# Early rows of a fourth expert, with weight loads and zero writes moved, in a fused attention and mixture-of-experts kernel

## The chip, the cores and the metric

One core of a Trainium2 chip runs the kernel. The metric is device time in microseconds (us): the median of the runs shown. Engines are called as the profile calls them: PE (matrix multiplication), DVE (vector), ACT (activations), POOL (GpSimd, which also issues the indirect transfers and those that change the data type) and SP (the sync engine, which issues plain transfers and nothing else here).

## What is computed

Linear attention over 8 batches of 576 tokens with 8 heads of 64, and on its output a layer of eight experts with noisy top-2 routing:

```python
phi = lambda x: np.where(x > 0, x, np.exp(x) - 1.0) + 1.0
q_p, k_p = phi(q), phi(k)
kv = np.einsum('bhsd,bhse->bhde', k_p, v);  z = np.sum(k_p, axis=2)
x = np.einsum('bhsd,bhde->bhse', q_p, kv) / (np.einsum('bhsd,bhd->bhs', q_p, z)[..., None] + 1e-06)
# x as 4608 tokens of 512
noisy = x @ w_gate + np.log1p(np.exp(x @ w_noise)) * noise     # 8 experts
top2, top2_w = two largest per token, softmax of the two
for e in range(8):                                             # w1[e] 512x1024, w2[e] 1024x512
    out[mask] += top2_w[mask] * (np.maximum(x[mask] @ w1[e], 0.0) @ w2[e])
```

## The kernel before

**Attention and routing.** Attention goes over four groups of two batches (g = 0 to 3). For each group the loads of q, k and v run on POOL's queue with a change to bf16 (`PhaseA.load`, L163); `exp` and `phi` make the features on ACT and DVE, `kv_mm` and `num` are the two products on PE. The tokens of a group are a routing unit; group 3 makes two, so there are five units (`UNITS`, L32). `rt_a`, `rt_b`, `rt_c` compute the two experts of every token, the weights and a row number, on DVE mostly.

**The lists.** Every expert has two lists of rows in a DRAM tensor, `x_sorted`: F, the tokens that visit it first (the lower of their two experts), and S, those that visit it second. `dispatch` (L391) writes the rows there: for each column of 128 tokens and each of the two experts one indirect transfer on POOL (L398), with a small memset behind it that keeps them apart (L389). That is 18 transfers for each of the units 0 to 2, 12 for unit 3 and 6 for unit 4. An F row's result goes to a tensor `part` (L661, on SP's queue); an S row's result is added to what `part` holds of the same token, gathered by POOL (L613, tile L), and scattered to the output (L667).

**Blocks.** The expert work is cut into tiles of 128 rows and blocks of one to four tiles. A block's rows are loaded on SP's queue (`xn_load`, L566, and a small `meta_load`, L449), transposed on PE (`xn_t`, L592) and copied by ACT (L596, L598); `mm1` (L630) makes the first product, in eight parts of 4 matmuls, ACT applies the relu (L632), and `mm2` (L645) the second, tile by tile; DVE scales the result (L649, L651). `interval` (L677) interleaves one block's first product with the second products of the block before and the transposes of the block after; behind it stand the gathers of L for the next block and, on POOL, the weight loads given to it (`w_load`, L442, one of the two matrices of an expert at a time). Each expert but the first and last also has 192 middle rows, at the border between its lists, whose place is known only at the end: `mid_gather` (L499) fetches them with two indirect transfers on POOL (L504, tile xm). M stands for these tiles in the plan.

**Early rows.** A list is complete only when unit 4 is dispatched. To have work for PE before, `ROUNDS` (L34) names, for three points (after units 0, 1 and 2), how many rows of the F lists of the first experts are full by then: at each point `rt_c` (L385) raises the row counters to these bounds, so that rows below them are never written later. Blocks below a bound are read as soon as the dispatches of that unit have landed: a load for round i takes the group number i (`early`, L550). Before the change the blocks are, in order, 0F0,2 in round 0; 0F2,2 and 1F0,3 in round 1; 0F4,2, 1F3,2 and 2F0,4 in round 2 (expert, list, first tile, number of tiles). Then comes c0, 0F6,4, the first block that needs the complete list, and the rest as in `PLAN` (L927).

**Orders.** The program is written out in the order in which every engine takes its instructions: `attention` (L758) has the groups and the first early blocks, `routing` (L883) the others, the kernel's main function (L939) the rest: at block i it prepares the expert of block i + 2 (`prepare`, L526: row data and the middle gather), loads rows two blocks ahead, and gives the weight loads of the table `todo` (L989) to the intervals. Weights lie in pools of two, three and one experts. Before the main loop nothing stands in PE's order but what these functions list.

**Zeros.** Some rows behind the lists are read without having been written; `attention` writes zeros there at its beginning, with seven transfers to `x_sorted` and two to `part` on SP's queue (L771 to L778).

Of the kernel before, what the change touches and what calls it, by code (L numbers as in the profile page):

```python
# [9 lines left out]
INT32 = mybir.dt.int32  # L10
# [23 lines left out]
ROUNDS = [(0, (256, 0, 0)), (1, (512, 384, 0)), (2, (768, 640, 512))]  # L34
EARLY = 3
# [14 lines left out]
def build_constants(tc, consts, w_gate, w_noise, noise):  # L50
# [23 lines left out]
    c["gap2"] = tile_("gap2", [P, 352])  # L74
# [337 lines left out]
class PhaseB:  # L412


    def __init__(self, ctx, tc, w1, w2, x_sorted, part, out):
# [11 lines left out]
        self.left, self.ready = [0] * 6 + [1] * 5 + [2] * 4, set()  # L427
# [16 lines left out]
    def meta_load(self, e, kind, i0, nt, group=None):  # L444

        m = self.mp.tile([P, nt, 4], INT32, name=f"meta{nt}{kind}")
# [310 lines left out]

def attention(pa, pb, c, x_sorted, zrow):  # L758
# [12 lines left out]
    nc.vector.memset(zrow[:], 0.0)  # L771

    for e, kind, i, n in ((0, "F", 8, 2 * P), (3, "F", 4, P), (4, "S", 4, P), (7, "S", 8, 2 * P), (E, "S", 0, 1)):
        row = pb.row(e, kind, i)
        for a in range(0, n, P):
            nc.sync.dma_start(out=x_sorted[row + a : row + min(n, a + P), :], in_=zrow[0 : min(P, n - a)])
    nc.sync.dma_start(out=pb.part[NO_P : NO_P + 1].bitcast(INT32)[:, 0 : ROW_W // 2], in_=zrow[0:1])
    nc.sync.dma_start(out=pb.part[NO_P : NO_P + 1].bitcast(INT32)[:, HD - ROW_W // 2 : HD], in_=zrow[0:1])  # L778
# [25 lines left out]
    for g in range(3):  # L804
# [4 lines left out]
        pa.phi(n, "k")  # L809
        if g < 2:  # L810
            pa.load(g + 2, "q")
# [42 lines left out]
        elif g == 1:  # L854
            for i in range(2):
                pa.dispatch(1, 3 * i, 3 * i + 3)
                pb.w_load(1, i)
            pa.dispatch(1, 6, 9)
            pb.xn_load(a1, 1)
            pb.meta_load(0, "F", 2, 2, 1)  # L860
            pb.meta_load(1, "F", 0, 3, 1)
        else:
            pa.dispatch(2)
# [19 lines left out]
def routing(pa, pb, c, first):  # L883
# [3 lines left out]
    a2, c0 = pb.block(2, ("F", 0, 4)), pb.block(0, ("F", 6, 4))  # L887
    pb.w_tiles(2, 1)
    pb.w_tiles(3, 1)
    pb.xn_load(a1, 1)  # L890
    pb.meta_load(0, "F", 4, 2, 2)
# [3 lines left out]
    pb.meta_load(2, "F", 0, 4, 2)  # L895
    pb.xn_load(a2, 2)
# [6 lines left out]
    pa.dispatch(3, 0, 3)  # L903
    pb.w_load(2, 0)
    pa.dispatch(3, 3, 6)
    pb.w_load(2, 1)
# [7 lines left out]
    pa.dispatch(4)  # L914
    pb.mids()
    pb.xn_t(b0, 0)
    pb.interval(b0, a1, (), b1)
    pb.prepare(0)
    pb.xn_load(c0)
    pb.interval(b1, b0, (), a2)  # L920
    pb.interval(a2, b1, (), c0)
    return a2, c0
# [123 lines left out]
```

## Time and profile before

| | |
|---|---|
| median of 9 runs | 448.85 us (442.62 to 453.0) |
| the profiled execution's own time | 447.72 us |
| its span, first to last instruction | 445.9 us |
| PE busy | 365.0 us, 82% of the span |
| POOL busy | 273.4 us, 61% |
| ACT, DVE busy | 194.1 us (44%), 183.6 us (41%) |
| mean granted clock of TensorE | 0.895 |
| first product, L630 | 832 matmuls, 150.0 us |
| second product, L645 | 640 matmuls, 147.4 us |
| dispatches, L398 | 72, 75.5 us of POOL |
| 16 weight loads, L442 | 1 MB each, 11.5 us from issue to landing (median) |

The profile is of one execution. Busy time is the time in which an engine works on an instruction; a time in the timelines counts from the first instruction. A line such as "b<-xt,w" names tiles by the program: the result is left of the arrow. The brackets behind an instruction of the timeline hold the idle time of its engine just before it and what ended it. A transfer has two times: the issue by its queue's engine, and the landing, when its semaphore tells that the data is there.

### The profile page before, as it was taken

How to read it: one execution, taken by the hardware profiler on the slowest of the kernel's cores; microseconds unless marked ns; L12 is line 12 of the kernel's file. 1: busy time of each engine (PE TensorE's matmuls, PEld its weight loads, DVE VectorE, ACT ScalarE, POOL GpSimd, SP SyncE). 2: the span in 40 equal slices, each digit the busy share in tenths (PEclk: the TensorE clock that was granted, in tenths of full speed). 3: DMA queues.
4: the chain of work that ended last, by engine and by line, in shares of the span. 5: the costliest groups of instructions: out<-in, count | busy, mean ns of one | idle time of the engine just before them, and what ended most of it. 6: DMA issues, size and time to landing. Idle time of an engine off the chain costs nothing.

```text
span 445.9 us, 7157 instructions
## 1 busy us (share of the span) xinstructions
PE 365.0 (82%) x2641; PEld 218.2 (49%) x2641; DVE 183.6 (41%) x471; ACT 194.1 (44%) x321; POOL 273.4 (61%) x408
## 2 busy tenths in 40 slices
PE   3593576474868779899999999799999899999990
PEld 1383465353645446445565445444645555554450
DVE  2746989998485722103423132312321141231230
ACT  1718654650624424353455534354444345445310
POOL 7120328988888887620084728268569846878781
PEclk9758856756788969999999999999999999999996
DMA  9999996599885399693387997977996996654440
GB/s 133 208 233 208 208 208 165 122 230 219 188 211 188 99 263 257 201 224 98 125 201 197 219 235 175 259 219 182 248 220 207 238 228 196 220 156 148 160 154 29
DMA packets 63010, 85.59 MB, mean 192 GB/s; under 512 B 15887, under 2 KB 45714, under 8 KB 62966
## 3 DMA queue, kind: packets, MB, share of 16 engines
q0 software_dynamic: 36160, 63.91, 64.6%
q1 hardware_dynamic: 25142, 20.96, 15.4%
q10 hardware_dynamic: 1664, 0.18, 0.5%
q8 instruction: 22, 0.36, 0.3%
q14 instruction: 22, 0.18, 0.1%
HBM read 83.88 MB, written 33.79 MB: 264 GB/s over the span
## 4 chain that ended last, share of the span: by engine, by line
PE 54%; DMA 21%; POOL 11%; DVE 6%; issue 4%; ACT 3%; POOLq 0%; SPq 0%; ACTq 0%; DVEq 0%
PE b L645 25%; PE b L630 24%; POOL x_sorted L398 7%; DMA kq<-in_q_dram 6%; DMA xm<-x_sorted,m_idx 5%; DMA xn<-x_sorted 4%; PE t L592 4%; DMA w<-in_moe_w_dram 3%; DMA kq<-in_k_dram 2%; POOL gap L389 2%; ACT e L178 1%; DMA x_sorted<-xr,posi 1%; ACT xt L596 1%; DVE e L190 1%; DVE xr L283 1%
## 5 line engine op out<-in xcount | busy, mean ns | idle before, releaser
L630 PE MATMUL b<-xt,w 128*128 128x256 bf16 (+5 forms) x832 | 150.0, 326 | 4.8 <-ACT xt L596 3.5
L645 PE MATMUL b<-w,hT 128*128 128x512 bf16 (+1 forms) x640 | 147.4, 386 | 0.0
L632 ACT ACTIVATE hT<-b 128x256 bf16<-128x256 f32 (+5 forms) x208 | 98.5, 484 | 101.4 <-PE b L630 99.1
L630 PEld LDWEIGHTS <-w 128*128 128x128 bf16 x832 | 79.8, 99 | 60.1 <-issue 9.2
L645 PEld LDWEIGHTS <-hT 128*128 128x128 bf16 (+1 forms) x640 | 59.7, 100 | 66.2 <-issue 5.7
L398 POOL DMA_INDIRECT x_sorted<-xr,posi x72 | 75.5, 1049 | 23.8 <-issue 11.9
L596 ACT COPY xt<-t 128x1024 bf16<-128x1024 bf16 x30 | 30.4, 1012 | 53.2 <-PE t L592 53.0
L613 POOL DMA_INDIRECT L<-part,mgi x12 | 12.0, 998 | 54.7 <-DMA xn<-x_sorted 30.9
L667 POOL DMA_INDIRECT out_dram<-y,si x34 | 33.7, 991 | 15.7 <-DVE y L649 11.5
L178 ACT ACTIVATE e<-kq 128x2304 bf16<-128x2304 bf16 x16 | 33.3, 2123 | 22.1 <-PE misc L209 9.3
L613 POOL DMA_INDIRECT L<-part,gi x34 | 34.7, 1020 | 6.9 <-issue 5.4
L209 PEld LDWEIGHTS <-e 64*128 64x128 bf16 x288 | 22.3, 128 | 17.3 <-DVE e L190 13.1
L209 PE MATMUL b<-v,e 64*128 64x192 bf16 x144 | 20.8, 323 | 8.9 <-DVE e L190 5.8
L592 PE MATMUL t<-ident,xn 128*128 128x128 bf16 (+1 forms) x256 | 21.0, 221 | 6.8 <-DMA xn<-x_sorted 5.7
L272 PE MATMUL num<-kvbd,pqt 128*64 128x162 bf16 x288 | 17.8, 294 | 10.4 <-DVE lwt L290 9.6
L209 PE MATMUL misc<-v,e 64*128 64x192 bf16 x144 | 20.7, 323 | 5.5 <-DMA v<-in_v_dram 5.5
L592 PEld LDWEIGHTS <-xn 128*128 128x128 bf16 (+1 forms) x256 | 17.2, 99 | 15.6 <-DMA xn<-x_sorted 7.0
L283 DVE TENSOR_TENSOR xr<-num,rden 128x768 bf16<-128x768 f32 x24 | 21.9, 952 | 2.2 <-DMA x_sorted<-xr,posi 1.5
L667 POOL DMA_INDIRECT out_dram<-y,msi x12 | 11.7, 976 | 16.3 <-DVE y L649 8.6
L190 DVE TENSOR_TENSOR e<-e,kq 128x2304 bf16<-128x2304 bf16 x16 | 21.5, 1357 | 0.3
L651 DVE TENSOR_SCALAR y<-b,meta2F 128x512 f32<-128x512 f32 x14 | 10.4, 749 | 27.0 <-PE b L645 26.9
L272 PEld LDWEIGHTS <-pqt 128*64 128x64 bf16 x288 | 14.9, 143 | 13.0 <-DVE lwt L290 7.6
(170 smaller groups left out, 358.8 us busy)
## 6 DMA issues: line engine op xcount, KB each, us to landing
w<-in_moe_w_dram POOLq DMA_DIRECT2D x16, 1024.0 KB, 11.5
part<-y SPq DMA_DIRECT2D x39, 256.0 KB, 3.6
kq<-in_k_dram POOLq DMA_DIRECT2D x8, 576.0 KB, 20.1
kq<-in_q_dram POOLq DMA_DIRECT2D x8, 576.0 KB, 13.1
v<-in_v_dram POOLq DMA_DIRECT2D x8, 576.0 KB, 23.0
xn<-x_sorted SPq DMA_DIRECT2D x11, 256.0 KB, 4.6
xn<-x_sorted SPq DMA_DIRECT2D x6, 384.0 KB, 4.6
xn<-x_sorted SPq DMA_DIRECT2D x4, 512.0 KB, 7.2
```

What stands on the lines that cost most here:

```text
L178: self.nc.scalar.activation(out=e, in_=x, func=ACT.Exp)
L209: nc.tensor.matmul(out=self.kvps[g, h, j][:, KVM * i : KVM * i + KVM], lhsT=e[half, hp, ci, :], rhs=v[half, hp::4, 64 * ci : 64 * ci + 64] ...
L272: nc.tensor.matmul(out=ps[half, hp, KVW * i : KVW * i + KVW], lhsT=self.pqt[g, 3 * t + i][:, hp, half], rhs=self.kvbd[g][:, j, hp, :], sta ...
L283: nc.vector.tensor_tensor(out=_ap(xr, [[64, 4], [ROW_W, 3], [1, 64]], off=3 * t * ROW_W + 256 * s), in0=_ap(ps, [[512, 4], [KVW, 3], [1, 6 ...
L398: r = self.nc.gpsimd.indirect_dma_start(out=self.x_sorted, out_offset=bass.IndirectOffsetOnAxis(ap=self.r["posi", u][:, ci - c0, sl : sl + ...
L592: nc.tensor.transpose(ps[:, i, dc, 0:m], self.xn(b, t, dc), self.c["ident"][0:m, 0:m])
L596: nc.scalar.copy(out=b["xt"][:, :, t * P : t * P + 2 * P].rearrange("p c (i r) -> p i c r", i=2), in_=ps)
L613: r = nc.gpsimd.indirect_dma_start(out=L[0:m].bitcast(INT32), out_offset=None, in_=self.part.bitcast(INT32), in_offset=bass.IndirectOffset ...
L630: nc.tensor.matmul(out=ps[:, 0:n], lhsT=w1[:, dc, fc * P : fc * P + P], rhs=b["xt"][:, dc, 0:n], start=(dc == 0), stop=(dc == 3))
L632: nc.scalar.activation(out=b["hT"][:, fc, 0:n], in_=ps[:, 0:n], func=ACT.Relu)
L645: nc.tensor.matmul(out=ps[i * m : i * m + m], lhsT=b["hT"][:, f, t * P : t * P + m], rhs=w2[:, f, :], start=(fc == 0), stop=(fc == 8 // n ...
L667: r = nc.gpsimd.indirect_dma_start(out=self.out, out_offset=bass.IndirectOffsetOnAxis(ap=self.m[e, kind, i]["si"][0:m], axis=0), in_=y[0:m ...
```

## The change

It does these things:

- Round bounds for a fourth expert: 256 rows of expert 2 in round 1 already, and 384 of expert 3 in round 2.
- The early blocks after 1F0,3 become 2F0,2 (round 1), 0F4,2, 1F3,2, 2F2,2 and 3F0,3 (round 2). The block 2F0,4 is split in two, and the first three tiles of expert 3 move from behind the blocks of expert 2 to a place ahead of c0. Expert 3's plan loses a 4-tile block and has 3F3,2, then M,S,M, then S1,2.
- The loads of rows for 2F0,2 and 0F4,2, 1F3,2 are issued on SP ahead of the stores of `routing`, as the early loads were; those for 2F2,2 and 3F0,3 stand ahead of the stores of the intervals.
- c0's preparation and row load stand behind the interval of 2F2,2; its transposes stand behind the interval of 3F0,3 and not inside it.
- Weight loads on POOL: expert 1's move from between the dispatches of unit 1 to between those of unit 2, expert 2's from between those of unit 3 to unit 2 too, expert 3's from the first intervals of the main loop to between the dispatches of unit 4. In the main loop each load of experts 4 to 7 comes with the blocks of the expert three below it, where it was two.
- The zeros are written in group 0 behind the features of k of group 1.
- The memset between indirect transfers of the second part is 416 words wide, where it was 352; that between dispatches stays at 192.

```diff
-ROUNDS = [(0, (256, 0, 0)), (1, (512, 384, 0)), (2, (768, 640, 512))]
-EARLY = 3
+ROUNDS = [(0, (256, 0, 0, 0)), (1, (512, 384, 256, 0)), (2, (768, 640, 512, 384))]
+EARLY = 4
...
-    c["gap2"] = tile_("gap2", [P, 352])
+    c["gap2"] = tile_("gap2", [P, 416])
...
-        m = self.mp.tile([P, nt, 4], INT32, name=f"meta{nt}{kind}")
+        m = self.mp.tile([P, nt, 4], INT32, name=f"meta{nt}{kind}" if group is None else f"early{e}_{i0}")
...
+def zeros(pb, x_sorted, zrow):
+    nc = pb.nc
+    nc.vector.memset(zrow[:], 0.0)
+
+    for e, kind, i, n in ((0, "F", 8, 2 * P), (3, "F", 4, P), (4, "S", 4, P), (7, "S", 8, 2 * P), (E, "S", 0, 1)):
+        row = pb.row(e, kind, i)
+        for a in range(0, n, P):
+            nc.sync.dma_start(out=x_sorted[row + a : row + min(n, a + P), :], in_=zrow[0 : min(P, n - a)])
+    nc.sync.dma_start(out=pb.part[NO_P : NO_P + 1].bitcast(INT32)[:, 0 : ROW_W // 2], in_=zrow[0:1])
+    nc.sync.dma_start(out=pb.part[NO_P : NO_P + 1].bitcast(INT32)[:, HD - ROW_W // 2 : HD], in_=zrow[0:1])
...
@@ attention: the same lines removed behind wblk @@
...
         pa.phi(n, "k")
+        if g == 0:
+            zeros(pb, x_sorted, zrow)
...
         elif g == 1:
-            for i in range(2):
-                pa.dispatch(1, 3 * i, 3 * i + 3)
-                pb.w_load(1, i)
-            pa.dispatch(1, 6, 9)
+            pa.dispatch(1)
...
         else:
-            pa.dispatch(2)
+            for i in range(2):
+                pb.w_load(1, i)
+                pa.dispatch(2, i, i + 1)
+            pa.dispatch(2, 2, 5)
...
@@ routing @@
-    a2, c0 = pb.block(2, ("F", 0, 4)), pb.block(0, ("F", 6, 4))
+    a2, b2 = pb.block(2, ("F", 0, 2)), pb.block(2, ("F", 2, 2))
+    a3, c0 = pb.block(3, ("F", 0, 3)), pb.block(0, ("F", 6, 4))
     pb.w_tiles(2, 1)
+    pb.w_load(2, 0)
+    pa.dispatch(2, 5, 7)
+    pb.w_load(2, 1)
+    pa.dispatch(2, 7, 9)
     pb.w_tiles(3, 1)
     pb.xn_load(a1, 1)
+    pb.meta_load(2, "F", 0, 2, 1)
+    pb.xn_load(a2, 1)
     pb.meta_load(0, "F", 4, 2, 2)
     pb.xn_load(b0, 2)
     pb.meta_load(1, "F", 3, 2, 2)
     pb.xn_load(b1, 2)
-    pb.meta_load(2, "F", 0, 4, 2)
-    pb.xn_load(a2, 2)
...
-    pa.dispatch(3, 0, 3)
-    pb.w_load(2, 0)
-    pa.dispatch(3, 3, 6)
-    pb.w_load(2, 1)
+    pa.dispatch(3)
...
-    pa.dispatch(4)
+    pa.dispatch(4, 0, 1)
+    pb.w_load(3, 0)
+    pa.dispatch(4, 1, 2)
+    pb.w_load(3, 1)
+    pa.dispatch(4, 2, 3)
     pb.mids()
-    pb.xn_t(b0, 0)
-    pb.interval(b0, a1, (), b1)
+    pb.xn_t(a2, 0)
+    pb.meta_load(2, "F", 2, 2, 2)
+    pb.xn_load(b2, 2)
+    pb.meta_load(3, "F", 0, 3, 2)
+    pb.xn_load(a3, 2)
+    pb.interval(a2, a1, (), b0)
+    pb.interval(b0, a2, (), b1)
+    pb.interval(b1, b0, (), b2)
+    pb.interval(b2, b1, (), a3)
     pb.prepare(0)
     pb.xn_load(c0)
-    pb.interval(b1, b0, (), a2)
-    pb.interval(a2, b1, (), c0)
-    return a2, c0
+    pb.interval(a3, b2, (), None)
+    pb.xn_t(c0, 0)
+    pb.xn_t(c0, 1)
+    return a3, c0
...
-    3: [[("F", 0, 4)], [("F", 4, 1), ("M", 0, 1), ("S", 0, 1), ("M", 1, 1)], [("S", 1, 2)]],
+    3: [[("F", 3, 2)], [("M", 0, 1), ("S", 0, 1), ("M", 1, 1)], [("S", 1, 2)]],
...
-        todo = {0: (3, 0), 1: (3, 1)}
-        for e in range(2, E - 2):
-            at = [i for i, b in enumerate(blocks) if b["e"] == e][:2]
+        todo = {}
+        for e in range(4, E):
+            at = [i for i, b in enumerate(blocks) if b["e"] == e - 3][:2]
             for k, i in enumerate(at):
-                todo[i] = (e + 2, k)
+                todo[i] = (e, k)
```

More of the change, by code (lines that the diff above doesn't have):

```diff
@@ L425, in __init__ @@
         self.w, self.m, self.x = {}, {}, {}
-        self.left, self.ready = [0] * 6 + [1] * 5 + [2] * 4, set()
+        self.left, self.ready = [0] * 6 + [1] * 5 + [2] * 4 + [3] * 3, set()
     def rot(self, pools, what):
@@ L770, in attention @@
     nc.vector.tensor_copy(out=wblk[64:P, :, 16:32], in_=wst[64:P])
[L771 to L778, printed above, removed]
     pa.rest()
@@ L1008 @@
                 e2, k = todo[i]
-                if k == 0 and e2 > 3:
+                if k == 0:
                     pb.w_tiles(e2, {4: 1, 5: 2}.get(e2, 0))
```

## The prediction

> **What bounds the kernel now.** I read the slices of the page first, then the waits of TensorE, then the timelines of PE and POOL around those waits, and last the DMA issues.
>
> ```profile
> PE   3593576474868779899999999799999899999990
> POOL 7120328988888887620084728268569846878781
> PEclk9758856756788969999999999999999999999996
> DMA  9999996599885399693387997977996996654440
> ```
>
> One digit is 11.1 us. From slice 17 (190 us) on PE is full but for three dents; before that it is not, while POOL is full from 64 to 182 us. So the end is set by when PE becomes full, and by what it still waits for afterwards.
>
> ```profile
> PE t L592 <- DMA xn<-x_sorted: 5.7, 3, 2.6
> PE t L592 <- DMA xm<-x_sorted,m_idx: 4.9, 2, 3.3
> PE b L630 <- ACT xt L596: 3.5, 4, 1.1
> ```
>
> These waits of PE (line, releaser, us in total, times, longest) are what an order of the expert work can win or lose: rows of the lists that come late (three times), middle rows gathered late (twice), transposed rows not yet copied. Where the first lies:
>
> ```profile
> 157.64 1.04 PE L592 MATMUL t<-ident,xn 128*128 128x128 bf16 x8 [2.61 <-DMA xn<-x_sorted]
> 159.77 1.86 PE L630 MATMUL b<-xt,w 128*128 128x256 bf16 x8 [1.10 <-ACT xt L596]
> 161.43 3.40 PE L645 MATMUL b<-w,hT 128*128 128x512 bf16 x8
> 164.67 1.04 PE L630 MATMUL b<-xt,w 128*128 128x256 bf16 x8
> ```
>
> PE has nothing from 155.0 to 157.6 (block 0F4,2 needs the table of round 2), and then runs at half speed: eight matmuls of 512 columns take 3.40 us here and 1.89 (1.73 start to start) later. Two more such waits are 1.94 us at 188.8 (the complete list of expert 0) and 1.13 us at 201.0.
>
> ```profile
> 160.90 0.82 POOL L442 DMA_DIRECT2D w<-in_moe_w_dram  x1
> 162.03 0.99 POOL L398 DMA_INDIRECT x_sorted<-xr,posi  x1 [0.30 <-issue]
> ...
> 170.24 0.96 POOL L442 DMA_DIRECT2D w<-in_moe_w_dram  x1
> 173.37 1.00 POOL L398 DMA_INDIRECT x_sorted<-xr,posi  x1 [2.17 <-ACT hT L632]
> ...
> 185.22 1.05 POOL L504 DMA_INDIRECT xm<-x_sorted,m_idx  x1 [3.56 <-DMA x_sorted<-xr,posi]
> ```
>
> On POOL a dispatch takes 1.40 us and a weight load 1.15, one after the other without a gap. The eighth DMA behind a weight load waits: 173.37 is the eighth after 160.90, and at 99.92 and 106.13, the eighth after the loads at 88.26 and 92.00, the timeline names the load itself (0.25 and 1.25 us). So POOL cannot run more than eight DMAs past a load that hasn't landed.
>
> ```profile
> w<-in_moe_w_dram POOLq DMA_DIRECT2D x16, 1024.0 KB, 11.5
> x_sorted<-xr,posi POOLq DMA_INDIRECT x72, 5.2
> xm<-x_sorted,m_idx POOLq DMA_INDIRECT x12, 9.6
> ```
>
> A load lands 9.9 to 15.2 us after its issue (median 11.5, last column), 10.4 where little else moves. What is issued behind it lands behind it: the gather below took 12.6 us, the one at 185.22, with no load ahead, 4.0.
>
> ```profile
> 272.00 0.85 POOL L442 DMA_DIRECT2D w<-in_moe_w_dram  x1
> 273.15 1.06 POOL L504 DMA_INDIRECT xm<-x_sorted,m_idx  x1 [0.30 <-issue]
> ```
>
> ```profile
> 285.83 0.40 PE L592 MATMUL t<-ident,xm 128*128 128x128 bf16 x4 [3.29 <-DMA xm<-x_sorted,m_idx]
> ```
>
> This is the middle gather of expert 4, and PE stands 3.29 us for it. I think it is the place that decides this change.
>
> **The change, part by part.** The profiled execution took 447.7 us (span 445.9 and 1.8 around it), 1.1 below the median of nine, 448.85. I add the terms to 447.7 and then move the sum to the median.
>
> *Dispatches and weight loads on POOL.* Without the two loads in them the 18 dispatches of unit 1 end at 125.0 instead of 127.1 (two times 1.15). Behind them come 18 dispatches of unit 2 and four loads (both of expert 1, both of expert 2): 18 x 1.40 + 4 x 1.15 = 29.8, and about 1.7 because the eighth DMA behind the second load (issued 129.0) comes before that load has landed (141.6, a load 4 us behind another took 13.9 at 92.00). The loads of expert 2 go out at 143.2 and 150.0, the last dispatch of unit 2 at 155.4 (151.31 now). It lands behind the load of 150.0: 150.0 + 10.4 + four dispatches of 0.4 = 162.0, where now it is 153.8. Meta and row loads of block 0F4,2 follow as now, 0.5 and 3.3 us: rows at 165.8. Unit 3 and 4 with expert 3's two loads: last issue 182.9 (now 180.4), last load issued 180.3 and landed about 193, the list complete at 194 to 197, block c0's rows 4.5 us later, 198.5 to 201.5.
>
> *PE from 155.0 to the first matmul of c0 (now 193.3, so 38.2 us).* A tile of 128 rows costs 1.73 us in the first product, 1.73 in the second, 0.23 in transposes; widths scale (0.87, 1.30, 1.51, 1.73 us for eight matmuls of 256, 384, 448, 512), so splitting blocks costs nothing in PE. New order a2, b0, b1, b2, a3: 11 tiles of first product 19.0, 11 of second 19.0, transposes of 14.5 tiles 3.3: 41.3 us. Idle: 1.1 for the copy of a2's rows (rows of round 1, there since 143, so the 2.61 and the half clock go); PE reaches b0's transposes at 156.6 + 0.87 + 1.73 + 0.87 + 1.73 = 161.8 and the rows come at 165.8: 4.0 new (bounds: 0 if the load lands in 9.9 and PE is late, 8.9 if it takes 15.2 as at 279.26); c0's transposes, now after the interval and no longer inside one, 0.45 + 1.05 + 0.33 + 0.95 less their work 0.8: 2.0; c0's rows themselves are there at about 200.8, when PE wants them (0 to 3). Sum 48.4, that is 10.2 longer. In exchange three tiles of expert 3 are done (3 x 3.69 = 11.1) and one second product less is pending (1.7): 12.8. Net -2.6.
>
> *Sync queue.* Ten issues of early rows at 0.4 to 0.5 us stand ahead of the stores; stores wait for the table at 162 as they do now at 154 (part<-y at 157.0), with nine output buffers nobody waits for it; cost 0. Cover gone, PE would wait for a store to land, 3.6 us (median of part<-y). The 1.13 us at 201.0 goes: the row load issued at 190.83 took 10.2 us beside expert 3's load of 188.2, which is now earlier: -1.1.
>
> *Zeros.* Nine DMAs go from 18.3 to about 44.7. Load q1 came at 43.4 and ScalarE waited 1.77 us for it; it would come some 3 us sooner. But VectorE, the next in the chain, was idle only 0.46 us before the dependent step at 47.64, and the memset adds 0.30 there. All loads behind have the same bytes ahead of them, and no engine waits for them later. Taken as 0 (bounds -1.5 and +0.3).
>
> *The middle gather of expert 4.* Let T be the end of the interval of the block that begins expert 3's rest (now 260.5). On POOL, what follows is the same before and after: gathers of L when expert 2's last store has landed (now 267.48, T+7.0), three of them, a weight load at T+11.5, the gather at T+12.7, landed by T+25.3 now. PE wants it now at T+22.0 (282.5). After, the intervals in between are shorter: block M,S,M (320 columns) 4.33 + two second products 3.46 + transposes 0.45 = 8.2, then in the next interval 0.87 + 1.73 + 0.87 + 1.73 + 0.45 + 0.87 + 0.98 + 0.22 = 7.7: wanted at T+15.9. With a landing between T+22 and T+25.3, taken T+23.9 since fewer stores run beside it, PE waits 8.0 instead of 3.29: +4.7 (bounds +2.5 and +6.1). The three tiles moved away were its cover. Two gaps in this computation are alike: expert 3's own gather is now behind two loads back to back, landing about 15 us after them (14.7 at 250.02), T1+26, and wanted at T1+32 (T1 the end of block 1F5,2): 0.
>
> *The clock after that wait.* This trace has both ends:
>
> ```profile
> 158.00:165.00 7.00, 5.90 (x27) 0.54 0.96 282
> 282.00:287.00 5.00, 1.71 (x18) 1.00 1.09 299
> ```
>
> (stretch, its length, PE busy, granted clock, DMA share, GB/s.) Waits of 2.61 and 1.10 us close together were followed by seven us at half clock; 3.29 us left it at 1.00. Eight us is beyond the first: half of seven us less what the wait covers, +2.7 (bounds 0 and 3.4). The Trainium skill, TensorE: Matmul & The Clock Gate, section HAM oscillation (how this bites in real kernels), has the rule that speaks against this change: no idle gaps on PE over about 3.4 us. By its window of 3.4 us the price would be 1.7 and the sum 1.0 lower; the seven us of this trace decide for me.
>
> *Later loads.* Loads come one expert earlier, so none lies ahead of expert 6's gather (344.88 and 355.37 now): the 1.61 us at 355.4 goes: -1.6. Expert 5's keeps its place (0 to 1). *The longer memset* (416 for 352 words; 192 take 276 ns, 352 take 409) adds 53 ns to 103 steps on POOL, idle there except near the end: +0.1 (bounds 0 and 1.5).
>
> Sum: -2.6 - 1.1 + 0 + 4.7 + 2.7 - 1.6 + 0.1 = **+2.2**: 449.9 in this execution's terms, **451.1** against the median.
>
> Another rule, the fit in DMA: Bandwidth & Descriptors, section Anatomy of one DMA (SWDGE path), gives about 4.4 us for a transfer of 1 MB. By it the gather would land near T+18, the wait would be shorter than now, and the sum about -7; the 9.9 to 15.2 us of this trace speak against it.
>
> **Rivals.** *A, faster: the gather of expert 4 is no later for PE than now.* Then 4.7 and 2.7 fall away: -5.2, 443.7. For it: the gather at 185.22 landed in 4.0 us. Against it: five gathers behind a load took 8.3 to 12.6. It decides if the gather lands before T+19.2. *B, slower: round 2's rows come far later.* The four dispatches behind expert 2's second load land with it; if that load takes 15.2 us, b0's wait is 8.9 and the clock falls there too: +4.9 and +3.4, 459.4. For it: four loads in 30 us instead of two. Against it: 10.4 and 10.5 us for loads beside dispatches alone. From 2.3 us more than my 4.0 it is slower by over 1%. *C, the change is nearly hidden:* the same, but the gather costs only its lower end and the clock holds: -2.6 - 1.1 + 2.5 - 1.6 + 0.1 = -2.7, 446.2. For it: 3.29 us did not throttle.
>
> **How the numbers follow.** Mine 0.42 (its own range 448 to 455), A 0.18, C 0.20, B 0.14, else 0.06. About 1%, 4.5 us, is what a measurement of this kernel can tell from no change. Below 444.4 lie most of A and a little of the rest, 0.19; above 453.3 lie B, the upper third of mine and half of the rest, 0.31; between, 0.50. Eight in ten need A's middle and most of B: 443 to 458.
>
> **What would show it.** Right: no PE wait near 157; a wait of 3 to 5 us for xn near 162 to 166; first matmul of c0 between 201 and 206; a wait for xm of 6 to 9.5 us in the second interval after block 3F3,2, then half clock; none before expert 6's middle rows. Wrong: that wait under 3.3 us, or a load landing in under 8; a wait for c0's rows over 3 us; POOL the last to end.

## The result and the profile after

The changed kernel takes 452.69 us (median of 10 runs, 451.03 to 454.0), the kernel before 446.42 (31 runs): ratio 1.0152, 95% interval 1.0118 to 1.0185. Beside a later group of runs it was 452.53 against 448.0, ratio 1.0126 (1.0073 to 1.0179). Ratios and intervals here go by the fast runs alone, so they differ a little from the quotients of the medians. The forecast was 451.1 and a small loss of 2.2 us; the loss is two to three times as large (6.3 and 4.5 us). The profiled execution has a span of 452.1 us, 6.2 more than that of before.

The slices of the page of the changed kernel, one digit is 11.3 us:

```profile
PE   3493576563766889998999999499999999999990
POOL 7120328888887888250008575658658878667982
PEclk9758856666879699998999999889999999999996
DMA  9999996597389998972338999996996666644541
```

PE has a hole in slice 25 (283 to 294 us) with a lower clock in it and behind it; the lowest clock of the expert work is in slice 13 (147 to 158 us), and slice 18 (203 to 215) has a dip. DMA is full in slices 12 and 13, where before it was at 5 and 3 tenths.

The waits of PE, as shown of before:

```profile
PE t L592 <- DMA xm<-x_sorted,m_idx: 5.7, 1, 5.7
PE t L592 <- DMA xn<-x_sorted: 3.3, 1, 3.3
PE b L630 <- ACT xt L596: 3.3, 3, 1.1
PE t L592 <- ACT xt L596: 2.2, 3, 1.1
```

One wait for rows is left instead of three, one for middle rows instead of two, each longer. PE's timeline has the first at a place that the forecast did not name:

```profile
139.76 3.92 PE L630 MATMUL b<-xt,w 128*128 128x256 bf16 x29
147.00 0.61 PE L592 MATMUL t<-ident,xn 128*128 128x128 bf16 x8 [3.32 <-DMA xn<-x_sorted]
...
149.09 6.30 PE L645 MATMUL b<-w,hT 128*128 128x512 bf16 x16
...
163.87 1.03 PE L630 MATMUL b<-xt,w 128*128 128x256 bf16 x8 [1.10 <-ACT xt L596]
164.74 1.89 PE L645 MATMUL b<-w,hT 128*128 128x512 bf16 x8
...
169.07 0.61 PE L592 MATMUL t<-ident,xn 128*128 128x128 bf16 x8
```

At 147.00 are the transposes of block 1F0,3. In the kernel before they ran at 142.61 without a wait, and the 16 matmuls behind them took 3.62 us, not 6.30. At 163.87 block 2F0,2 has only its 1.10 us for the copy, and block 0F4,2 (169.07) waits for nothing: the 2.61 us of before are gone, and the 4.0 us that the forecast put there did not come, because PE gets there 7 us late.

Why are the rows of 1F0,3 late? Their load was issued at 139.17 (before: 137.98). This is what the DMA queues moved in the four microseconds from 138 to 142, first before, then after (q0 is POOL's queue, q1 SP's; packets, MB, share of the 16 engines):

```profile
q1 hardware_dynamic: 544, 0.66, 54.7%
q0 software_dynamic: 121, 0.41, 28.6%
```

```profile
q0 software_dynamic: 615, 0.79, 97.6%
q1 hardware_dynamic: 298, 0.26, 25.9%
```

Before, POOL's queue carries dispatches alone, and SP's queue gets its store and the rows of 1F0,3 through. After, expert 1's second weight load (issued at 129.67; a dispatch waits 2.18 us for it until 142.86) fills the engines; behind it come the dispatches that were issued meanwhile. The store of 138.71, ahead of the rows on SP's queue, moves from 142 on, and the rows from 144 to 147.5.

The next loss is at block c0 (0F6,4), whose transposes now stand outside an interval:

```profile
204.91 0.61 PE L592 MATMUL t<-ident,xn 128*128 128x128 bf16 x8
206.62 0.60 PE L592 MATMUL t<-ident,xn 128*128 128x128 bf16 x8 [1.10 <-ACT xt L596]
208.17 2.24 PE L630 MATMUL b<-xt,w 128*128 128x448 bf16 x8 [0.95 <-ACT xt L598]
210.21 3.05 PE L645 MATMUL b<-w,hT 128*128 128x512 bf16 x8
213.09 1.68 PE L630 MATMUL b<-xt,w 128*128 128x448 bf16 x8
```

The rows are there and the two waits are the 2.0 us forecast, but the clock falls behind them: 2.24 and 3.05 us instead of 1.68 and 1.89, another 1.7.

The last is the middle gather of expert 4. POOL, then PE:

```profile
277.50 1.05 POOL L613 DMA_INDIRECT L<-part,mgi  x1 [4.25 <-DMA part<-y]
...
282.17 0.85 POOL L442 DMA_DIRECT2D w<-in_moe_w_dram  x1
283.32 1.05 POOL L504 DMA_INDIRECT xm<-x_sorted,m_idx  x1 [0.30 <-issue]
```

```profile
284.82 1.05 PE L645 MATMUL b<-w,hT 128*64 128x512 bf16 x8
285.81 0.40 PE L592 MATMUL t<-ident,xn 128*128 128x128 bf16 x4
291.90 0.61 PE L592 MATMUL t<-ident,xm 128*128 128x128 bf16 x4 [5.69 <-DMA xm<-x_sorted,m_idx]
292.30 5.33 PE L630 MATMUL b<-xt,w 128*128 128x256 bf16 x16
```

The gather again stands behind a weight load, PE waits 5.69 us instead of 3.29, and the 16 matmuls behind it (8 of 256 and 8 of 512 columns) take 5.33 us; at full speed they take 0.87 + 1.73 = 2.6. So 2.7 us go to the clock, the figure forecast.

Three marks on PE give the balance: the first transpose of expert 1's middle rows, that of expert 4's, and the last matmul.

| us on PE | to expert 1's middle rows | from there to expert 4's | from there to the last matmul |
|---|---|---|---|
| before | 213.2 | 72.6 | 147.9 |
| after | 226.7 | 65.2 | 147.9 |
| after, a second profile | 224.9 | 66.1 | 147.2 |
| loss of the change, moved work taken out | +2.4 (second: +0.6) | +2.7 (+3.6) | +1.0 (+0.3) |
| forecast | -3.7 | +4.7 | +1.2 |

The moved work: three tiles of 3.69 us, 11.1, go into the first column. Out of the second go only 10.1, since the second product of expert 3's half tile, 1.0 us, stands ahead of expert 4's mark now (at 284.82, above) and stood behind it before:

```profile
287.03 1.05 PE L645 MATMUL b<-w,hT 128*64 128x512 bf16 x8
```

So the third holds 1.0 less work than before. The forecast: -2.6 - 1.1 in the first, +4.7 in the second, +2.7 - 1.6 + 0.1 in the third.

### The profile page after: what moved, and what is told of

Its sections match the earlier page's. It is cut to its first block, busy times and chain, and to the rows that moved or that the text cites. A ratio compares the mean times of both kernels' runs of the same rounds, so it can differ in the third digit from the quotient of the medians.

```text
span 452.1 us, 7309 instructions
## 1 busy us (share of the span) xinstructions
PE 366.8 (81%) x2705; PEld 223.2 (49%) x2705; DVE 185.0 (41%) x474; ACT 196.2 (43%) x337; POOL 278.2 (62%) x408
## 4 chain that ended last, share of the span: by engine, by line
PE 55%; POOL 15%; DMA 13%; DVE 8%; ACT 4%; issue 4%; POOLq 0%; ACTq 0%; SPq 0%; DVEq 0%
PE b L645 24%; PE b L630 23%; POOL x_sorted L398 4%; DMA v<-in_v_dram 4%; PE t L592 3%; POOL L L613 3%; DMA x_sorted<-xr,posi 3%; POOL out_dram L667 3%; DMA part<-y 2%; DMA xm<-x_sorted,m_idx 2%; ACT xt L596 2%; DMA xn<-x_sorted 2%; POOL gap L620 1%; DVE xr L283 1%; PE misc L209 1%
## 5 line engine op out<-in xcount | busy, mean ns | idle before, releaser
L630 PE MATMUL b<-xt,w 128*128 128x256 bf16 (+5 forms) x896 | 152.1, 318 | 6.0 <-ACT xt L596 3.3
L645 PE MATMUL b<-w,hT 128*128 128x512 bf16 (+1 forms) x640 | 149.6, 390 | 0.0
L632 ACT ACTIVATE hT<-b 128x256 bf16<-128x256 f32 (+5 forms) x224 | 100.6, 461 | 101.7 <-PE b L630 98.5
L630 PEld LDWEIGHTS <-w 128*128 128x128 bf16 x896 | 86.7, 100 | 57.9 <-issue 11.7
L645 PEld LDWEIGHTS <-hT 128*128 128x128 bf16 (+1 forms) x640 | 60.6, 101 | 67.0 <-issue 10.2
L651 DVE TENSOR_SCALAR y<-b,early 128x512 f32<-128x512 f32 x18 | 13.5, 750 | 45.3 <-PE b L645 45.3
L272 PE MATMUL num<-kvbd,pqt 128*64 128x162 bf16 x288 | 16.4, 278 | 10.4 <-DVE lwt L290 9.7
L620 POOL MEMSET gap<- 128x416 f32 x46 | 21.2, 461 | 0.1
L504 POOL DMA_INDIRECT xm<-x_sorted,m_idx x12 | 12.4, 1031 | 13.9 <-DMA x_sorted<-xr,posi 11.1
## 6 DMA issues: line engine op xcount, KB each, us to landing
w<-in_moe_w_dram POOLq DMA_DIRECT2D x16, 1024.0 KB, 12.7
```

The source lines that it names most:

```text
L620: nc.gpsimd.memset(self.c["gap2"][:], 0.0)
L630: nc.tensor.matmul(out=ps[:, 0:n], lhsT=w1[:, dc, fc * P : fc * P + P], rhs=b["xt"][:, dc, 0:n], start=(dc == 0), stop=(dc == 3))
L632: nc.scalar.activation(out=b["hT"][:, fc, 0:n], in_=ps[:, 0:n], func=ACT.Relu)
L645: nc.tensor.matmul(out=ps[i * m : i * m + m], lhsT=b["hT"][:, f, t * P : t * P + m], rhs=w2[:, f, :], start=(fc == 0), stop=(fc == 8 // n ...
```

## The experiments

The theory from the profile after: the loss is made of a wait that expert 1's moved loads cause (3.3 us and as much clock at 147), of c0's transposes outside an interval, and of the gather behind a load. Rivals: the additional row load of 2F0,2 or expert 2's loads make the wait at 147; the gather is late for other reasons; the zeros cost something. Twelve kernels ran, four at a time. The second four ran beside a kernel before of 448.0 us; the first and the third four on another chip, where it takes 460.41 and 460.56. On which of the two the first comparison ran is not known for certain; its times (446.42 and 452.69) agree with those of the second four, so it is counted with that chip, called the first one here. A kernel is compared by its ratio to the kernel before beside it, and directly only with kernels of its own chip.

### First four: one edit each

`e1_loads_behind`, in the main loop (a block's load is issued in the turn of the next block, behind its `prepare`):

```diff
+        behind = None
...
-            parts = []
-            if i in todo:
-                e2, k = todo[i]
+            if behind:
+                e2, k = behind
                 if k == 0:
                     pb.w_tiles(e2, {4: 1, 5: 2}.get(e2, 0))
-                parts = [(e2, k)]
-            pb.interval(b, prev, parts, nxt)
+                pb.w_load(e2, k)
+            behind = todo.get(i)
+            pb.interval(b, prev, (), nxt)
```

> The changed kernel with one thing else: in the blocks behind the early ones, a weight load is issued behind the gather of middle rows that falls into the next block's turn instead of ahead of it (the loads of experts 4 to 7). My theory, that the gather for expert 4 is late because it stands behind the load of 282.17: the gather goes out at about 282.2 and lands in 4 to 6 us, at 286 to 288; TensorE, which wants it at 286.2, waits 0 to 2 us instead of 5.69, the half clock behind it (16 matmuls of 512 columns in 5.33 us) goes, and the time falls by 6 to 8 us, to 445 to 447 us, about level with the kernel before. Rival, that the gather is late because it is issued late (it stands behind the three gathers of part rows, which wait for a store until 277.5) and the load has little to do with it: a wait of 4 us or more stays, and the time falls by 1 to 2 us at most.

`e2_w1_back`:

```diff
-            pa.dispatch(1)
+            for i in range(2):
+                pa.dispatch(1, 3 * i, 3 * i + 3)
+                pb.w_load(1, i)
+            pa.dispatch(1, 6, 9)
...
-            for i in range(2):
-                pb.w_load(1, i)
-                pa.dispatch(2, i, i + 1)
-            pa.dispatch(2, 2, 5)
+            pa.dispatch(2, 0, 5)
```

> The changed kernel with the two weight loads of expert 1 back between the dispatches of unit 1. Theory 1, that these loads (125.95 and 129.67) delay the rows of block 1F0,3 to 147 and the delay covers the wait for block 0F4,2's rows that I had forecast: the wait of 3.32 us at 147 and the half clock behind it go (6 us), but TensorE then reaches block 0F4,2 at 162 to 163 while its rows land at 165 to 167, so that 2 to 5 us of wait appear there, with some half clock; in all the time falls by 0 to 4 us, to 449 to 453 us. Theory 2, that the delay at 147 is a plain loss and nothing waits behind it: the time falls by 6 us, to 446.5. Rival, that the additional row load of block 2F0,2 on the sync queue delays 1F0,3's rows and the weight loads do not: the wait at 147 stays at about 3 us and the time is the changed kernel's, 452 to 453.

`e3_zeros_back` has the call of `zeros` ahead of `pa.rest()` again.

> The changed kernel with the zeros written where they were, ahead of the later loads of the attention stage. If the move of the zeros cost the 0.7 us by which the first dispatch and the 1.7 us by which the rows of block 0F0,2 are later in the changed kernel's profile, the first dispatch is back at 64.4 and the time is 1 to 1.7 us lower, 451 to 452. My forecast's term, that the move is worth nothing: the changed kernel's time within 0.5 us. Rival, that the move helps as intended: 1 to 1.5 us higher, 454.

`e4_c0_inside`:

```diff
-    pb.interval(a3, b2, (), None)
-    pb.xn_t(c0, 0)
-    pb.xn_t(c0, 1)
+    pb.interval(a3, b2, (), c0)
```

> The changed kernel with the transposes of block 0F6,4 back inside the interval of block 3F0,3, as in the kernel before. Theory: the two waits of 1.10 and 0.95 us for the copies of the transposes and the slower clock behind them (8 matmuls of 448 columns in 2.24 and 8 of 512 in 3.05 us instead of 1.68 and 1.89) go, since the rows, issued at 196.23, are there at about 201: 3 to 4 us lower, 448.5 to 450. Rival 1, that the rows are not there at the first place inside the interval: a wait for xn of 1 to 3 us takes their place and the time is within 1 us of the changed kernel's. Rival 2, that the lower clock there has another cause than the two waits: only 1.5 to 2 us lower, 451.

| kernel | us | ratio to before | 95% interval |
|---|---|---|---|
| e1_loads_behind | 455.21 | 0.9898 | 0.9849 to 0.9947 |
| e2_w1_back | 477.23 | 1.0362 | 1.0308 to 1.0416 |
| e3_zeros_back | 460.83 | 1.0032 | 1.0004 to 1.0059 |
| e4_c0_inside | 456.93 | 0.994 | 0.9901 to 0.998 |

The gather first. POOL with the load ahead (e4), and with it behind (e1), and PE of both:

```profile
287.27 0.85 POOL L442 DMA_DIRECT2D w<-in_moe_w_dram  x1
288.43 1.05 POOL L504 DMA_INDIRECT xm<-x_sorted,m_idx  x1 [0.30 <-issue]
```

```profile
290.18 1.02 POOL L504 DMA_INDIRECT xm<-x_sorted,m_idx  x1 [0.16 <-PE b L645]
...
293.22 0.85 POOL L442 DMA_DIRECT2D w<-in_moe_w_dram  x1
```

```profile
295.84 0.61 PE L592 MATMUL t<-ident,xm 128*128 128x128 bf16 x4 [5.62 <-DMA xm<-x_sorted,m_idx]
```

```profile
294.57 0.40 PE L592 MATMUL t<-ident,xm 128*128 128x128 bf16 x4 [1.78 <-DMA xm<-x_sorted,m_idx]
```

From issue to use it is 7.4 us behind a load and 4.4 ahead of it, at the same place of the same program on the same chip. That the gather is late because of the load is shown, and the rival (4 us of wait stay) falls. In e4 the two waits at c0 are gone, and no wait for its rows takes their place; how much clock goes with them shows on the first chip only, below: on this one the two waits, still there in e1, left the clock alone.

e2 did the opposite of all that was expected: 3.6% slower than before. The wait for 1F0,3's rows did not go (6.71 us at 156.86), and another is far longer, on PE and, where it begins, on DVE:

```profile
126.05 1.10 PE L272 MATMUL num<-kvbd,pqt 128*64 128x162 bf16 x24 [1.32 <-DVE lwt L290]
138.36 1.83 PE L272 MATMUL num<-kvbd,pqt 128*64 128x162 bf16 x24 [11.21 <-DVE lwt L290]
```

```profile
128.08 0.75 DVE L651 TENSOR_SCALAR y<-b,early 128x512 f32<-128x512 f32 x1 [2.09 <-PE num L272]
135.30 0.18 DVE L279 TENSOR_SCALAR rden<-num 128x24 f32<-128x24 f32 x1 [6.47 <-remote]
```

The PE result that DVE reads at 135.30 was there at 127.15; "remote" means that the profile finds nothing in the program that let DVE go. This chip has several such halts and the first has not: ACT stands 6.64 us with the same word at the copy for block 2F0,2 in e3, and PE waits 8.44 there. What they are stays open. Nor do the traces show instructions being loaded then: no packet of the instruction queues moves from 119 to 139 us in e2, or from 161.5 to 169 in e3. So e2's time cannot say what the wait at 147 would be on the first chip; what its wait of 6.71 us says of the rows comes with the third four.

e3: the ratio is at no place that speaks for a cost of the zeros. The changed kernel itself did not run on this chip. If the two repairs act independently, its ratio is that of e1 (0.9898) times that of e4 (0.994) over that of both together (0.9837, below): 1.000, an estimate; against it e1 gains 4.7 us and e4 2.8, where 6 to 8 and 3 to 4 were expected. The first chip's traces say more of the zeros: PE begins the transposes of block 0F0,2 at 109.87 before, and at 111.56 and 109.81 in two profiles of the changed kernel, so the later start in the first of them was that execution's. The zeros are worth nothing that these runs can see.

### Second four: the repairs together, and one on the kernel before

`after_again` is the changed kernel.

> The changed kernel itself, beside the kernel before on one chip, as the base for the variants of this call and, with the first four, for a second chip. If its loss lies in the order of instructions and not in one chip's transfer times, the ratio to the kernel before is 1.012 to 1.019, as in the first comparison; if the loads of expert 2's weights land late here too (the first matmul of block 2F0,2 waited 4 to 8 us in the first four kernels, against 1.10 us for the copy in the changed kernel's first profile), it is above 1.02; the wait for expert 4's middle rows is 5 to 6 us in either case.

`e5_behind_inside` has the edits of e1 and e4.

> The changed kernel with two edits together: the later weight loads behind the gather of middle rows, and the transposes of block 0F6,4 inside the interval of block 3F0,3. Theory: the two losses lie in different stages and add up: 4 us of wait and 2 to 3 us of slower clock at expert 4's middle rows, and 2 us of wait and 1.7 us of slower clock at the first matmul of block 0F6,4, so 8 to 11 us below the changed kernel, and 1 to 4 us below the kernel before (ratio to it 0.990 to 0.998). Rival: what the second gains is given back at the first, since TensorE comes to it 3 to 4 us earlier: then only 6 us below the changed kernel, level with the kernel before.

`e6_before_behind` has the edit of e1 made in the kernel before, and nothing of the change.

> The kernel before with one part of the experiments alone: its weight loads behind the gather of middle rows (those of experts 4 to 7). Theory: the waits of 3.29 us (expert 4) and 1.61 us (expert 6) go, and nothing else moves: 3 to 5 us faster than the kernel before, ratio 0.989 to 0.993, so that this gain does not belong to the change. Rival: the load behind it then comes late for its expert, or the gather is late anyway: within 1 us of the kernel before.

`e7_gather_early` has the edit of e4, the loads where the change has them, and

```diff
-        if 0 < e < E - 1:
+        if 0 < e < E - 1 and e not in self.x:
...
+            if i + 3 < len(blocks) and 4 <= blocks[i + 3]["e"] < E - 1 and blocks[i + 3]["e"] not in pb.x:
+                pb.mid_gather(blocks[i + 3]["e"])
```

> The changed kernel with the transposes of block 0F6,4 inside as above and the weight loads where they were, but the gather of middle rows of experts 4 to 6 issued one block earlier, ahead of the gathers of part rows that wait for a store. Theory: what makes the gather late is its place behind that wait and the load; one block earlier it lands long before TensorE wants it: no wait for middle rows at all, 1 to 2 us faster than with the loads behind it (which left 1.78 us of wait and some slow clock). Rival: the gather earlier only makes other transfers late, the part rows above all: as with the loads behind it, or slower.

| kernel | us | ratio to before (448.0 us) | 95% interval | PE marks as above |
|---|---|---|---|---|
| after_again | 452.53 | 1.0126 | 1.0073 to 1.0179 | 224.9, 66.1, 147.2 |
| e5_behind_inside | 443.05 | 0.9909 | 0.987 to 0.9948 | 221.8, 61.2, 146.7 |
| e6_before_behind | 440.97 | 0.9887 | 0.9836 to 0.9938 | 212.0, 69.2, 146.1 |
| e7_gather_early | 442.88 | 0.9899 | 0.985 to 0.9949 | 223.4, 60.6, 145.4 |

The changed kernel's ratio is as expected, and its wait for expert 4's middle rows 6.34 us. The two repairs together take 9.5 us from it, as forecast for them (8 to 11). The stage of c0 in e5:

```profile
203.02 0.61 PE L592 MATMUL t<-ident,xn 128*128 128x128 bf16 x8
203.56 2.99 PE L630 MATMUL b<-xt,w 128*128 128x384 bf16 x16
206.38 1.89 PE L645 MATMUL b<-w,hT 128*128 128x512 bf16 x7
208.11 1.68 PE L630 MATMUL b<-xt,w 128*128 128x448 bf16 x8
```

No wait, full clock. From 1F0,3's transposes to the second eight matmuls of c0 it is 62.1 us here and 66.0 in after_again (145.31 to 211.28): 3.8 less, the 2.0 of waits and 1.8 of clock. The second column falls by 4.9, of which 4.5 are the wait for expert 4's rows (6.34 to 1.80).

e6 is the fastest kernel of the study: 7.0 us below before (3 to 5 were expected), and faster than the changed one by 11.6. In it the wait of 3.29 us is gone:

```profile
280.98 0.39 PE L592 MATMUL t<-ident,xn 128*128 128x128 bf16 x4
281.20 0.39 PE L592 MATMUL t<-ident,xm 128*128 128x128 bf16 x4
```

So is the one of 1.61 us at expert 6, and the 1.13 us at 201 too, since the edit moves expert 3's loads too, which the expectation did not count: that of its first matrix goes out at 191.61 (188.21 before), behind the row load of 191.00 that it held up. These three waits are 6.0 of the 7.0 us. That gain does not belong to the change: with the gather ahead of the load in both, the change is at 443.05 against 440.97, and the intervals overlap. By the marks, moved work taken out as above, e5 is 1.3 us ahead of e6 in the first column in spite of its wait at 147, and loses 2.1 and 1.6 in the other two, where it still waits 1.80 us for expert 4's rows and runs slower behind that.

e7 has no wait for middle rows at all and is no faster than e5: PE waits 1.12 us for S rows one block earlier.

```profile
281.33 0.62 PE L592 MATMUL t<-ident,xn 128*128 128x128 bf16 x8 [1.12 <-DMA xn<-x_sorted]
...
283.98 0.39 PE L592 MATMUL t<-ident,xm 128*128 128x128 bf16 x4
```

The expected 1 to 2 us did not come; whether the earlier gather makes those rows late was not tried.

### Third four: the wait at 147

`e11_base_again` is e5 again, the base on this chip.

> The changed kernel with the two repairs alone (later weight loads behind the gather of middle rows, transposes of block 0F6,4 inside the interval), the base for the others of this call: ratio to the kernel before 0.987 to 0.995, as the first time.

`e8_w1_early` is e5 with the edit of e2.

> The changed kernel with the two repairs (later weight loads behind the gather of middle rows, transposes of block 0F6,4 inside the interval) and, a third edit, expert 1's weight loads back between the dispatches of unit 1. It is read against the two repairs alone, run beside it. Theory 1, the wait of 3.3 us at 145 to 147 for block 1F0,3's rows and the 2 to 3 us of slower clock behind it are made by expert 1's loads, and they cover the wait for block 0F4,2's rows that the forecast had: the first goes, TensorE reaches block 0F4,2's transposes at 162 to 163, the rows come at 163 to 166, so 1 to 4 us of wait are back there and perhaps slow clock; net 1 to 4 us faster. Theory 2, nothing waits behind it: 5 to 6 us faster, no wait for rows near 162. Rival, the loads of expert 2 or the additional row load make the wait: it stays at 3 us or more, and the time is unchanged.

`e9_w2_late` is e5 with

```diff
-    pb.w_load(2, 0)
     pa.dispatch(2, 5, 7)
+    pb.w_load(2, 0)
+    pa.dispatch(2, 7, 8)
     pb.w_load(2, 1)
-    pa.dispatch(2, 7, 9)
+    pa.dispatch(2, 8, 9)
```

> The changed kernel with the same two repairs, and the two weight loads of expert 2 two and three dispatches (2.8 and 1.4 us) later. If the load of expert 2 at 143 is what holds back block 1F0,3's rows (issued at 138 to 139, landed at 145 to 147, while the DMA share was 1.10), the wait there shrinks from 3.4 to 1 us or less and the time falls by 2 to 5 us. If expert 1's loads and the dispatches behind them do it, the wait stays at 3 us or more and the time stays within 1 us, or rises where the first matmul of block 2F0,2 now waits for the weights.

`e10_before_w1_late` is the kernel before with

```diff
-            for i in range(2):
-                pa.dispatch(1, 3 * i, 3 * i + 3)
-                pb.w_load(1, i)
-            pa.dispatch(1, 6, 9)
+            pa.dispatch(1)
...
-            pa.dispatch(2)
+            for i in range(2):
+                pb.w_load(1, i)
+                pa.dispatch(2, i, i + 1)
+            pa.dispatch(2, 2, 9)
```

> The kernel before with one part of the change alone: expert 1's two weight loads behind the dispatches of unit 1, with the first dispatches of unit 2 between them, as in the changed kernel. There is no load of expert 2 near and no additional row load. Theory: the wait of about 3 us for block 1F0,3's rows at 145 to 147 appears here too, with slow clock behind it; the wait of 2.6 us for block 0F4,2's rows at 157.6 shrinks by as much as TensorE comes later; in all 2 to 4 us slower than the kernel before. Rival, that the load of expert 2 or the additional row load is what delays these rows: no wait there, and the kernel before's time within 1 us.

| kernel | us | ratio to before (460.56 us) | 95% interval |
|---|---|---|---|
| e11_base_again | 451.67 | 0.9837 | 0.9785 to 0.989 |
| e8_w1_early | 466.25 | 1.0109 | 1.0038 to 1.0181 |
| e9_w2_late | 449.89 | 0.9783 | 0.9718 to 0.9848 |
| e10_before_w1_late | 453.28 | 0.9819 | 0.975 to 0.9888 |

These ran on the slower chip, and there the move of expert 1's loads is the good part of the change. Alone it takes 7.3 us from the kernel before (e10, where 2 to 4 us of loss were expected); undone in the repaired kernel, where 1 to 6 us of gain were expected, it takes the ratio from 0.9837 to 1.0109 (e11 and e8), as in e2. By what way it costs so much is not shown: e2 and e8 have the most time in halts of the kind described above (22.8 and 37.3 us; e11 13.9), and the kernel before was not profiled on this chip. The theory of the wait, as it was put for these runs, is not confirmed by them. In e10 PE comes to 1F0,3's transposes at 147.69, 5 us later than on the first chip, and waits for nothing, so that rows landing by 147.5 are not late there.

```profile
147.26 0.60 PE L630 MATMUL b<-xt,w 128*128 128x256 bf16 x4 [0.86 <-issue]
147.69 0.61 PE L592 MATMUL t<-ident,xn 128*128 128x128 bf16 x8
```

In e9, with expert 2's load at 150.64 instead of 144.31, PE gets these rows no sooner (transposes at 148.12 behind a wait of 0.89 us; in e11 at about 148.2, behind a first product and without a wait). Its own time against e11 is within the intervals.

On the first chip all four profiles with expert 1's loads late (after, after_again, e5, e7) wait 3.3, 3.5, 3.4 and 4.5 us for 1F0,3's rows, and both with them early (before, e6) wait none. The profiles of both chips fit one picture when they are put in order by how long ahead of this row load the last weight load was issued:

| profile | weight load ahead by, us | rows, from issue to PE's use | PE's wait for them |
|---|---|---|---|
| e2 (expert 2's load) | 3.6 | 10.3 | 6.7 |
| e8 (expert 2's load) | 4.3 | 8.9 | 4.3 |
| e7 | 8.7 | 9.3 | 4.5 |
| after, after_again, e5 | 9.4 to 9.5 | 7.8 to 7.9 | 3.3 to 3.5 |
| e1, e3, e4, e9 | 11.0 | 5.0 to 5.8 | 0.9 to 1.6 |
| e10, e11 | 11.0, 11.8 | at most 5.0, 4.6 | none |
| before, e6 | 20 | at most 4.6, 4.3 | none |

The ends of the table, POOL and PE of e2, then of e1:

```profile
143.06 0.81 POOL L442 DMA_DIRECT2D w<-in_moe_w_dram  x1 [1.35 <-issue]
156.86 1.01 PE L592 MATMUL t<-ident,xn 128*128 128x128 bf16 x8 [6.71 <-DMA xn<-x_sorted]
```

```profile
131.73 0.95 POOL L442 DMA_DIRECT2D w<-in_moe_w_dram  x1
147.78 0.61 PE L592 MATMUL t<-ident,xn 128*128 128x128 bf16 x8 [0.85 <-DMA xn<-x_sorted]
```

So the rows are late where a weight load, of whichever expert, was issued less than 10 us ahead of them. On the slower chip they are issued later (141.5 to 143.6 us with expert 1's loads late), which puts them 11 us behind the load. The additional row load of 2F0,2, issued about 1.1 us behind these rows, is there in all kernels but before, e6 and e10: it alone does not make them late, since e1, e3, e4, e9 and e11 have it too. Nor does a weight load issued behind them: in e1 and e3 expert 2's follows after 1.9 us, in e9 after 7.6, and the rows take 5.0 to 5.1 in all three. This is read from profiles that differ in other things as well. Undoing the move of the weight loads on the first chip was not run, so its share there is argued, not shown by an experiment.

## Why the prediction was right or wrong

The direction and the range were right (451.1, 443 to 458; measured 452.69), the size of the loss was not: +2.2 against +6.3 between the medians and +6.2 between the spans (+4.5 by both in the second comparison). By the columns of the table of marks it was -3.7, +4.7 and +1.2 against +2.4, +2.7 and +1.0 (second profile +0.6, +3.6, +0.3): the first stretch has the wrong sign and the second is too dear, so that two errors partly cancel in the sum. That much of its nearness is luck. The direction rests on the middle gather and the clock behind it, whose mechanism the runs show. Of the signs named, no wait near 157, half clock behind expert 4's rows and none before expert 6's came; the wait near 162 to 166 did not, c0's first matmul came at 208.2 and 206.4 (201 to 206 was said), and the wait for expert 4's rows was 5.69 and 6.34 us (6 to 9.5).

*Dispatches and loads on POOL* were right to about a microsecond: loads of expert 2 issued at 144.03 and 150.56 (forecast 143.2 and 150.0), those of expert 3 up to 180.72 (180.3), the dispatch that waits for the load at 142.86, 2.18 us (1.7). The last dispatch of unit 2 landed at about 163 (162.0).

*PE from 155.0 to c0, -2.6,* is the step that failed; with the 1.13 us, which did go, it was to give -3.7 and gave +2.4 and +0.6. It failed in three places. First, the sum began at 155.0, the end of 1F0,3's first product, as if nothing ahead of it moved; but its rows come 4.4 us later, and the wait and the half clock make PE end there at 162.2: 3.3 + 2.7 = 6.0 us that no term had. The forecast did place expert 1's loads at 125 and 129 and did say that what stands behind a load lands behind it; it applied this to POOL's own queue and never to SP's, whose store and row load were crossing at that time. That the weight load is what holds them is argued from the queues and from the table of the third four. Secondly, the 4.0 us for 0F4,2's rows did not come, since PE gets there 7 us late. Thirdly, c0's transposes cost the 2.0 us of waits, and 1.7 of clock on top. -3.7 + 6.0 - 4.0 + 1.7 is 0.0, against +2.4 and +0.6; of the first, 1.7 is the start, which differs by so much between two profiles of one kernel, and some 0.7 us stays unexplained in both.

*The zeros, 0*: right as far as seen.

*The middle gather of expert 4, +4.7*: the mechanism was right, shown by e1, e5 and e6. The size was not: the stage lost 2.7 and 3.6 us, and the wait was 5.69 and 6.34 us, not 8.0, since the load landed in 9.3 us in the first profile and the gather was there at T + 21.9, not T + 23.9. PE wanted it at T + 16.2 (15.9 was forecast).

*The clock behind it, +2.7*: measured 2.7 (5.33 us for work of 2.6).

*Expert 6's gather, -1.6*: gone, as was the 1.13 us at 201. *The memset*: about 410 to 461 ns, some 50 as against 53.

Rival A (443.7, no later gather) is refuted for this program. e5 comes close to its time, 443.05, but has c0's transposes moved as well, worth 3.8 us, so that the nearness says little of A's price. Rival B had the right consequence, slower by over 1%, by other causes: the late rows were those of round 1, not round 2. Rival C's condition, that the clock holds, did not occur.

The Trainium skill has a rule that would have pointed to the missing term: DMA: Bandwidth & Descriptors, section Queues, rings and completion order, says that each DMA engine takes turns between the queue rows that have work, packet by packet. So SP's transfers share the engines with POOL's. The trace agrees: 97.6% and 25.9% of the 16 engines in the same four microseconds, and the row load of 384 KB took at most 4.6 us from issue to PE's use beside dispatches alone (before) and 7.8 beside the weights.

## What to carry to other kernels

When a bulk load is moved, look not only at what stands behind it on its own queue but at every transfer of the other queues in the 10 to 13 us until it lands (the medians of these profiles are 10.3 to 12.7), and begin the sum there. A small gather or row load that an engine will want goes ahead of a bulk load that nobody wants yet: putting the loads behind was worth 7.0 us in the kernel before, more than the whole change cost. And run an order on a second chip before calling it better: the same move of two loads gained 7.3 us on one and came with a new 3.3 us wait on another.

## What the runs showed of the hardware

The clock does not follow from the length of a wait alone. On one chip waits of 1.10 and 0.95 us 1.5 us apart were followed by half clock (after: 2.24 and 3.05 us at c0; after_again: 2.87 for the first eight), and behind one of 1.80 us (e5) nine matmuls took 2.34 us that take 1.1 at full speed, while the 3.29 us of the kernel before slowed none. On the other chip the same two short waits in e1 left the clock alone (8 matmuls of 448 columns in 1.67 us). The stretches behind expert 4's wait, before and after:

```profile
284.00:292.00 8.00, 6.17 (x39) 3.15 (x40) 4.33 (x11) 2.77 (x5) 2.96 (x5) 1.00 1.14 253
```

```profile
291.00:299.00 8.00, 7.10 (x27) 3.55 (x28) 3.35 (x9) 2.88 (x5) 4.33 (x6) 0.57 1.06 200
```

(The third number from the end is the granted clock.) The Trainium skill, TensorE: Matmul & The Clock Gate, in its part on the HAM clock gate, calls the window that decides a free-running one, so that the same idle time may or may not fill it; the unlike outcomes here fit that, and no run here shows the window itself. That 1.80 us were enough in e5 does not fit the rule of gaps over about 3.4 us which the prediction quotes; the measurement decides.

Two chips differ by 3% on one program (446 to 448 and 460 us), and not evenly: the move of expert 1's loads gains 7.3 us on the slower one, and goes with a new wait on the other, where it was not run alone. A 4608-byte packet takes 0.18 us in the median on either. What the slower chip's profiles have and the first chip's have not are halts of DVE and ACT of up to 8.8 us that the profile puts down to nothing in the program, with PE waiting behind them. Their cause, and whether they make up the whole difference, is open.
